# Experts by triples of feature blocks, converted weights kept in DRAM, pairs begun with four single blocks

## The chip, the cores and the metric

The kernel runs on one core of one Trainium2 chip. The metric is the device time of one execution in microseconds (us). Three executions of the kernel before took 2083.7 (median), 2082.83 and 2087.57 us.

## The reference

Three stages, of which the last is the one that changes:

```python
x = attention(r, k, v, w, u)          # 4 x 8 heads, 768 steps, 48 wide -> 3072 tokens x 384
x = (h * tanh(softplus(h))) @ w_out   # h = x @ w_in, 384 -> 2048 -> 384
logits = x @ w_gate                   # 8 experts
P = exp(logits - logits.max())
for _ in range(8):                    # rows, then columns, made to sum up evenly
    P /= P.sum(1, keepdims=True) + 1e-09
    P /= P.sum(0, keepdims=True) + 1e-09
    P *= N / E
for e in range(8):
    out += P[:, e:e + 1] * (relu(x @ w1[e]) @ w2[e])   # 384 -> 1024 -> 384
```

Everything is float32, and the output is 3072 x 384.

## The kernel before

Tokens lie in six tiles of 512, features on partitions: `xT[n]` holds a tile as three blocks (`KI`) of 128 features. The expert stage takes two tiles at a time, a pair q = 0, 1, 2. A float32 product of a 128 x 128 weight block and a 128 x 512 token block is made of three matmuls on parts of the operands (`PASSES`: high x high, high x low, low x high), so each operand is split first: ACT copies the rounded high part, POOL or DVE subtracts it from the source for the low part. In the middle of the program, therefore, every block of x and every weight exists as a high and a low tile.

Per pair, the hidden features of the eight experts (8 blocks of 128 each, 64 in all) are done in groups of two blocks (`groups`, 96 of them). The products of a group are 2 token tiles x 2 feature blocks x 3 input blocks, 12 by themselves; with sums of weights (`w_sums`, L797 to L800) and sums of x (`x_sum`) the group needs 11, in 8 steps, on two banks of PSUM, `U_` and `Bk` (`p1`, `prod`, L846). After each step the bank is read out: by ACT (`c_out`, L868) or by DVE with a sum (L871), with one sum on POOL (L873). Four finished hidden tiles per group are rectified and split, high by ACT (`c_hi`, L879), low by DVE (`c_lo`, L885).

The second layer's matmuls of the group before (`y_part`, L893) are issued between those steps: six after an even step, three after an odd one, into six more banks `Y`. At the end of an expert, DVE weights each of the six banks with that expert's P (L909; `pb` is P laid out over partitions) and POOL adds it to the output tile, which takes the place of x in `xT` (`y_out`, L910). Expert 0 of pair 0 is copied out unweighted (L903) since P is not ready, and weighted later (L1122).

Each group loads four raw weight tiles of 192 KB (`load_w`, L775, on SP's queue), in each pair anew. ACT and POOL split them (`w_hi` L784, `w2_hi` L804, `w_lo` L790). Between pairs, the nine blocks and sums of x are split anew (`x_split`, L840 on ACT and L841 on DVE), at steps of a table at the end of the builder. The order on every engine is the order of the calls in `step`: `step_pe` (products, the entries of `slot`, the second layer's matmuls) and then `step_rest` (weights of the next groups, read-outs, splits, outputs, the entries of `aux`).

The first group's steps are put between the last iterations of the mish layer (`lead`, `ready`), whose result is evacuated at L340. The logits of the last tile are made after that: three differences on DVE (L1088) give the low parts for its matmuls. After the last group come `tail_out` and `tail_turn`, which weight and turn the last two tiles.

## Time and profile before

| | |
|---|---|
| median of three executions | 2083.7 us |
| the profiled execution | 2087.63 us |
| its span | 2085.8 us |
| granted clock of TensorE, mean | 0.993 |
| busy: TensorE, DVE, ACT, POOL | 98%, 62%, 56%, 54% |
| mean rate of the DMA queues | 70 GB/s |

The profile is of one execution by itself, 3.9 us above the median; its own time stands beside its span, and the runs are compared with each other. In it PE is TensorE, DVE is VectorE, ACT is ScalarE, POOL is GpSimd, and SP issues the DMAs. A line such as L871 is a line of the kernel. The granted clock is the share of full speed that the chip allows TensorE in a stretch (1.00 is 2.4 GHz). The expert stage runs from about 549 us to the end.

### The profile page before, as it was taken

The numbers are of one execution on the slowest core, as the hardware profiler recorded it, in microseconds if no ns is written. First come the engines' busy times: TensorE is split into PE (matmuls) and PEld (weight loads), VectorE is DVE, ScalarE is ACT, GpSimd is POOL, SyncE is SP. The second block draws the span as 40 slices with busy tenths as digits, with TensorE's granted clock in tenths as the row PEclk, the third lists the DMA queues.
The fourth block names the chain that finished last, engine by engine and source line by source line (L and its number), as shares of the span: only waits on it lengthen the run. The fifth ranks groups of instructions, "written<-read, shape, count | busy, mean of one in ns | idle before, by whom it ended". The sixth has DMA issues, their size and how long they took to land.

```text
span 2085.8 us, 27895 instructions
## 1 busy us (share of the span) xinstructions
PE 2052.8 (98%) x9586; PEld 1695.8 (81%) x9586; DVE 1286.1 (62%) x2219; ACT 1167.5 (56%) x2486; POOL 1128.6 (54%) x979
## 2 busy tenths in 40 slices
PE   8899999999999999999999999999999999999998
PEld 7888888888788888888878888888878888888887
DVE  8988789778766555445574445555466454455554
ACT  7888888878644444444444555555544444444442
POOL 5546566446534665555564456555566455555651
PEclk8999999999999999999999999999999999999999
...
GB/s 255 211 141 29 33 23 46 16 1 16 25 51 63 67 60 48 62 64 64 56 68 97 96 94 90 101 76 87 93 56 90 64 50 56 65 62 60 60 50 47
DMA packets 127689, 145.56 MB, mean 70 GB/s; under 512 B 35056, under 2 KB 113584, under 8 KB 127536
## 3 DMA queue, kind: packets, MB, share of 16 engines
...
q14 instruction: 76, 0.62, 0.1%
HBM read 138.82 MB, written 4.82 MB: 69 GB/s over the span
## 4 chain that ended last, share of the span: by engine, by line
PE 92%; DVE 3%; ACT 2%; issue 1%; POOL 1%; DMA 0%; POOLq 0%; DVEq 0%; ACTq 0%
PE y L893 37%; PE Bk L846 21%; PE U L846 12%; PE ph L239 9%; PE x L324 9%; PE ya L643 1%; PE un L614 1%; PE sc L602 1%; ACT A L594 1%; PE ya L641 1%; DVE A L607 0%; DVE tc L871 0%; ACT xT L654 0%; POOL wc L790 0%; POOL g L313 0%
## 5 line engine op out<-in xcount | busy, mean ns | idle before, releaser
L893 PE MATMUL y<-g,w 128*128 128x512 f32 x3456 | 911.3, 390 | 0.0
L893 PEld LDWEIGHTS y<-g,w 128*128 128x128 f32 x3456 | 646.2, 188 | 140.7 <-DVE tc L909 7.3
L879 ACT ACTIVATE g<-tc 128x512 fp32r<-128x512 f32 x384 | 242.7, 632 | 651.3 <-DVE tc L871 651.3
L871 DVE TENSOR_TENSOR tc<-Bk,tc 128x512 f32<-128x512 f32 x288 | 199.0, 691 | 571.7 <-PE Bk L846 566.6
L790 POOL TENSOR_TENSOR wc<-er,wc 128x384 fp32r<-128x384 f32 x192 | 212.6, 1107 | 418.8 <-ACT wc L784 418.8
L885 DVE SCALAR_TENSOR_TENSOR g<-tc,g 128x512 fp32r<-128x512 f32 x384 | 309.3, 805 | 60.4 <-ACT g L879 59.8
L846 PE MATMUL Bk<-xc_X,wc 128*128 128x512 f32 x864 | 244.0, 390 | 0.6 <-POOL xc_X L841 0.6
L790 POOL TENSOR_TENSOR w<-er,w 128x384 fp32r<-128x384 f32 x192 | 210.4, 1112 | 56.5 <-ACT w L804 51.8
L324 PE MATMUL x<-g,wm 128*128 128x512 f32 x864 | 212.4, 390 | 0.4 <-POOL g L313 0.2
L239 PE MATMUL ph<-xs,wm 128*128 128x512 f32 x864 | 212.0, 390 | 0.3 <-POOL xs L209 0.3
L910 POOL TENSOR_TENSOR xT<-xT,tc 128x512 f32<-128x512 f32 x120 | 164.2, 1392 | 86.8 <-DVE tc L909 75.1
L873 POOL TENSOR_TENSOR tc<-tc 128x512 f32<-128x512 f32 x96 | 133.2, 1387 | 120.9 <-ACT tc L868 116.8
L239 PEld LDWEIGHTS ph<-xs,wm 128*128 128x128 f32 x864 | 161.8, 188 | 36.6 <-POOL xs L209 0.7
L846 PEld LDWEIGHTS Bk<-xc_X,wc 128*128 128x128 f32 x864 | 162.4, 188 | 35.5 <-POOL xc_X L841 1.0
L324 PEld LDWEIGHTS x<-g,wm 128*128 128x128 f32 x864 | 161.6, 188 | 35.8 <-POOL g L313 1.1
L313 POOL TENSOR_TENSOR g<-y,g 128x512 fp32r<-128x512 f32 x96 | 125.0, 1302 | 113.3 <-ACT g L308 106.6
L868 ACT ACTIVATE tc<-U 128x512 f32<-128x512 f32 x288 | 169.8, 590 | 26.7 <-PE U L846 21.5
L846 PE MATMUL U<-xh,wc 128*128 128x512 f32 x576 | 162.4, 390 | 0.6 <-DVE tc L871 0.6
L846 PE MATMUL Bk<-xc_B,wc 128*128 128x512 f32 x576 | 161.7, 389 | 0.0
L846 PEld LDWEIGHTS U<-xh,wc 128*128 128x128 f32 x576 | 108.1, 188 | 24.7 <-DVE tc L871 1.5
L846 PEld LDWEIGHTS Bk<-xc_B,wc 128*128 128x128 f32 x576 | 108.1, 188 | 22.5
L784 ACT ACTIVATE wc<-er 128x384 fp32r<-128x384 f32 x192 | 99.3, 517 | 45.0 <-DVE er L800 45.0
...
## 6 DMA issues: line engine op xcount, KB each, us to landing
er<-in_w_dram SPq DMA_DIRECT2D x384, 192.0 KB, 2.4
...
lt<-in_kr_dram SPq DMA_DIRECT2D x24, 384.0 KB, 5.7
raw<-in_w_in_dram SPq DMA_DIRECT2D x16, 384.0 KB, 3.3
raw<-in_w_out_dram SPq DMA_DIRECT2D x16, 384.0 KB, 3.1
seen<-in_w_in_dram SPq DMA_DIRECT2D x16, 384.0 KB, 3.5
seen<-in_w_out_dram SPq DMA_DIRECT2D x16, 384.0 KB, 3.2
```

Of the source, the lines that this page charges most:

```text
L239: pe.matmul(ph, w[:, pw, k, :], xs[:, px, :], start=(m == 0), stop=(m == 3 * KI - 1))
L313: pool.tensor_tensor(gs[i][:, 1], y, gs[i][:, 0].bitcast(F32), op=ALU.subtract)
L324: pe.matmul(sums[n][k], wo[f][:, pw, k, :], g[:, px, :], start=(f == f0 and m == 0), stop=(f == f1 and m == 1), skip_group_check=True)
L790: eng.tensor_tensor(flat(t[:, 1]), src, flat(t[:, 0]).bitcast(F32), op=ALU.subtract)
L846: pe.matmul(out_, w[:, pw, :], x[px], start=(start and m == 0), stop=(stop and m == 2), skip_group_check=True)
L868: act.activation(tt[("t0", "t5", "t2", 0, "t3")[s]], Bk if s == 1 else U_, AF.Copy)
L871: dve.tensor_tensor(t, U_ if s == 6 else Bk, t, op=ALU.add)
L873: pool.tensor_tensor(tt["t2"], tt["t2"], tt["t5"], op=ALU.add)
L879: act.activation(g[:, 0], tt[nm], AF.Relu)
L885: dve.scalar_tensor_tensor(g[:, 1], tt[nm], 0.0, g[:, 0].bitcast(F32), op0=ALU.max, op1=ALU.subtract)
L893: pe.matmul(Y[t][k], w2[G, f][:, pw, k, :], x[:, px, :], start=(g == 0 and f == 0 and m == 0), stop=(g == NGR - 1 and f == 1 and m == 2), ...
L910: pool.tensor_tensor(o, o, t_, op=ALU.add)
```

## The change

The 64 feature blocks of a pair are taken as four single blocks and twenty triples, without regard to where an expert ends (`groups`). A single block has 3 steps: 6 products without any weight sums (`T1`). A triple is 2 token tiles x 3 feature blocks x 3 input blocks in 15 products and 15 steps (`T3`): every product is one step, the two banks take turns, and each bank keeps adding up over its products, so that what is read out after a step is a partial sum. A row of `T3` names the product, whether its bank starts anew, how it is read out (c copied, n copied with its sign turned, both by ACT at L925; + and - added to or taken from a hidden tile by DVE at L927; L929 is that of the single blocks), and to which of the tiles. Six of the fifteen read-outs finish a hidden tile. Its low half (L1019) is not issued in its own step but in the next one, behind that step's read-out (`pend`). Five places are kept for hidden tiles.

The second layer's matmuls are given out as jobs of three (`job`, L1027) by a plan made when the kernel is built (`plan_jobs`): a smooth curve of jobs per step between what is finished two steps before and what must be done for a place to come free.

Weights are converted in pair 0 only. Every converted tile (high and low, 384 KB) is written to DRAM (`w_keep`, L855: eight for a triple, two for a single block, 168 in all) and read back for pairs 1 and 2 (`w_back`, L859, 336 loads). Sums of weights (`w_sums`, L820) are 10 DVE operations a triple.

The fifteen x operands need more room: two tiles of x are saved to DRAM and read back later, pair 2 is worked on in the first two tiles. The first three experts of pair 0 are written to DRAM without weights (L1047), read back in pair 1 and weighted and added on POOL. At a pair change the operands are made anew in an order of their own (`refill`, with `x_split` at L881 and L882 and `x_neg` at L889).

```diff
-NGR = NF2 // 2
+NB = E * NF2
+NSG = 4
+NTR = (NB - NSG) // 3
+GQ = NSG + NTR
+NPK = 3
+NGB = 5
...
-    XN = ("B11", "T1", "T2", "B21", "X31", "T3", "B22", "X32", "T4")
-    WN = ("A11", "A12", "A13", "S4", "A22", "A23", "S1", "S2", "S3")
-    groups = [(q, e, g) for q in range(NQ) for e in range(E) for g in range(NGR)]
...
+    T3 = ((14, 1, "c", "00"), (2, 1, "c", "21"), (12, 0, "c", "10"), (4, 1, "c", "11"), (13, 1, "+", "10"),
+          (7, 1, "-", "21"), (6, 0, "-", "11"), (1, 0, "-", "11"), (5, 0, "-", "21"), (0, 0, "+", "10"),
+          (11, 0, "n", "01"), (8, 0, "+", "00"), (9, 0, "+", "00"), (3, 0, "-", "01"), (10, 0, "c", "20"))
+    DONE = {7: "11", 8: "21", 9: "10", 12: "00", 13: "01", 14: "20"}
+    T1 = (((("a0", 5), ("a2", 1)), 1, "c", 1), ((("a0", 9), ("a1", 12), ("a2", 14)), 1, "-", 0), ((("a1", 4),), 0, "c", 1))
+    ROW = {"1": 0, "2": 1, "0": 2}
+    TI = {"00": 0, "21": 1, "10": 2, "11": 3, "01": 3, "20": 2}
+    groups = [
+        (q, fs) for q in range(NQ) for fs in [(f,) for f in range(NSG)] + [(f, f + 1, f + 2) for f in range(NSG, NB, 3)]]
...
+    def w_keep(G, i, second, t, z):
+        fs = groups[G][1]
+        d = kept[fs, i, second] = dr.tile([128, 2, KI, 128], F32, name=f"keep{fs[0]}_{i}_{int(second)}")
+        at_z(z, lambda: nc.sync.dma_start(d, t.bitcast(F32)))
+    def w_back(G, i, second):
+        if G < NGT:
+            nc.sync.dma_start(w_new(G, i, second).bitcast(F32), kept[groups[G][1], i, second])
...
+    def x_neg(o, x, y):
+        dve.scalar_tensor_tensor(o, x, -1.0, y, op0=ALU.mult, op1=ALU.subtract)
...
-    STEPS = ((("S1", "T1"),), (("A12", "B21"), ("A13", "X31")), (("S4", "B22"), ("A13", "X32")),
-             (("A22", "T4"), ("A23", "X31")))
-    STEPU = (("A11", "B11"), ("S2", "T2"), ("S3", "T3"), ("A23", "X32"))
...
+    banks, cnt, used = [None, None], [0], {}
+    def steps(G):
+        return T3 if full(G) else T1
     def p1(G, s):
+        b = banks[cnt[0] & 1]
+        sb[0] = banks[1 - (cnt[0] & 1)]
+        cnt[0] += 1
+        used[G, s] = b
+        if full(G):
+            p, start, _, _ = T3[s]
+            prod(b, G, p, p, start, True)
         else:
+            ps_, start, _, _ = T1[s]
+            for j, (wn, xn) in enumerate(ps_):
+                prod(b, G, wn, xn, start and j == 0, j == len(ps_) - 1)
+    def evac(G, s):
+        b = used.pop((G, s))
+        if full(G):
+            _, _, kind, o = T3[s]
+            t = tmp["c", TI[o]]
         else:
+            _, _, kind, o = T1[s]
+            t = tmp["c", 2 * (G % 2) + o]
+        if kind in "cn":
+            act.activation(t, b, AF.Copy, scale=1.0 if kind == "c" else -1.0)
+        elif full(G):
+            dve.tensor_tensor(t, t, b, op=ALU.add if kind == "+" else ALU.subtract)
+        else:
+            dve.tensor_tensor(t, b, tmp["c", 2 * (G % 2) + 1], op=ALU.subtract)
+        f = done_(G, s)
+        return (t,) + f if f else None
...
+    def c_hi(G, t, f, tok):
+        q = groups[G][0]
+        g = gfix[gslot[q, f, tok]]
+        act.activation(g[:, 0], t, AF.Relu)
+        gg[q, f, tok] = g
+        return lambda: dve.scalar_tensor_tensor(g[:, 1], t, 0.0, g[:, 0].bitcast(F32), op0=ALU.max, op1=ALU.subtract)
...
+        if q == 0 and e < NPK:
+            d = raws[e, t, k] = dr.tile([128, TT], F32, name=f"yraw{e}_{t}_{k}")
+            act.activation(t_, yo, AF.Copy)
+            nc.sync.dma_start(d, t_)
...
+        p1(G, s)
+        for fn in slot.pop((G, s), ()):
+            fn()
+        while jp[0] < jq[zi[G, s]]:
+            job(*jobs[jp[0]])
+            jp[0] += 1
...
+        done = evac(G, s)
+        for fn in pend:
+            fn()
+        pend.clear()
+        if done:
+            if gfix:
+                pend.append(c_hi(G, *done))
+            else:
+                early.append((G, *done))
...
+        on(0, 7, sp(13, "C", dve))
+        on(0, 8, sp(1, b[2][1], pool))
+        on(0, 9, sp(5, b[0][1], pool))
+        on(0, 10, lambda: x_neg(x_tmp("D"), tmp["C"], b[2][1]))
+        on(0, 10, sp(7, "D", dve))
+        on(0, 11, tt("A", b[1][0], "A", ALU.subtract))
+        on(0, 11, neg("D", "C", b[0][1]))
+        on(0, 12, sp(6, "D", dve))
+        on(0, 13, sp(9, "B", pool))
```

Three places in the order of instructions. First, TensorE in the steady part of a pair. Before, L846 is the first layer (U and Bk are its banks, `wc` weights, the others x) and L893 the second (y):

```order
L893 MATMUL y_5781<-g_5_7739,w_15_0_7599 128x512 x3
L846 MATMUL Bk<-xc_B_5395,wc_0_7675 128x512 x3
L846 MATMUL Bk<-xc_X_5435,wc_0_7675 128x512 x3
L893 MATMUL y_5782<-g_5_7739,w_15_0_7599 128x512 x3
L846 MATMUL U<-xc_T_5528,wc_2_7702 128x512 x3
L893 MATMUL y_5777<-g_7_7769,w_15_1_7617 128x512 x3
L893 MATMUL y_5778<-g_7_7769,w_15_1_7617 128x512 x3
L846 MATMUL Bk<-xc_B_5651,wc_1_7688 128x512 x3
L846 MATMUL Bk<-xc_X_5689,wc_0_7675 128x512 x3
```

After it, L895 is the first layer and L1027 a job of the second:

```order
L895 MATMUL U<-hB,wc_4_10144 128x512 x3
L1027 MATMUL y_5816<-gf_5820,w_0_10019 128x512 x3
L895 MATMUL Bk<-hC,wc_4_10144 128x512 x3
L1027 MATMUL y_5817<-gf_5820,w_0_10019 128x512 x3
L895 MATMUL U<-xc_5715,wc_3_10129 128x512 x3
L1027 MATMUL y_5812<-gf_5818,w_0_10019 128x512 x3
L895 MATMUL Bk<-xc_5759,wc_0_10105 128x512 x3
L1027 MATMUL y_5813<-gf_5818,w_0_10019 128x512 x3
L895 MATMUL U<-xc_5790,wc_4_10144 128x512 x3
L1027 MATMUL y_5814<-gf_5818,w_0_10019 128x512 x3
```

Between two uses of the same bank by different steps there were 12 or 15 matmuls of other work and there are now 9 or 12, and a bank is read out after three matmuls each time, where `Bk` mostly was after six.

Second, DVE at the hand-over from the mish layer (L340 and L347 read out its last result; L389, L392, L396 and L399 are the logits; L885 and L1019 low halves; L871 read-outs). Before:

```order
L340 TENSOR_TENSOR xT_78<-half_3501,x_4_8_0_5452 128x512
L340 TENSOR_TENSOR xT_78<-half_3501,x_4_8_1_5453 128x512
L340 TENSOR_TENSOR xT_78<-half_3501,x_4_8_2_5454 128x512
L389 STREAM_TRANSPOSE gt_5741<-g_4378 32x512
L392 TENSOR_TENSOR lg<-gt_5741 32x32 x4
L871 TENSOR_TENSOR tc_5576<-Bk,tc_5576 128x512
L871 TENSOR_TENSOR tc_5576<-U,tc_5576 128x512
L885 SCALAR_TENSOR_TENSOR g_5_5749<-tc_5576,g_5_5749 128x512
L871 TENSOR_TENSOR tc_5577<-Bk,tc_5577 128x512
L885 SCALAR_TENSOR_TENSOR g_6_5785<-tc_5576,g_6_5785 128x512
```

After it, L882 is a split of x and L1360 the gate differences:

```order
L347 TENSOR_TENSOR xT_92<-half_3505,x_4_8_0_5463 128x512
L347 TENSOR_TENSOR xT_92<-half_3505,x_4_8_1_5464 128x512
L347 TENSOR_TENSOR xT_92<-half_3505,x_4_8_2_5465 128x512
L396 STREAM_TRANSPOSE gt_5783<-g_4382 32x512
L399 TENSOR_TENSOR lg<-gt_5783 32x32 x4
L882 TENSOR_TENSOR xc_5790<-xt_D,xc_5790 128x512
L1019 SCALAR_TENSOR_TENSOR gf_5818<-tc_5629,gf_5818 128x512
L1019 SCALAR_TENSOR_TENSOR gf_5819<-tc_5630,gf_5819 128x512
L1019 SCALAR_TENSOR_TENSOR gf_5820<-tc_5631,gf_5820 128x512
L1019 SCALAR_TENSOR_TENSOR ge_5821<-tc_5632,ge_5821 128x512
L1360 TENSOR_TENSOR xg_1_5835<-xT_92,xg_0_5834 128x512
L1360 TENSOR_TENSOR xg_1_5839<-xT_92,xg_0_5838 128x512
```

A split, four low halves (`gf` and `ge` are the places of hidden tiles) and the gate differences now stand there in a row.

Third, DVE at the change from pair 0 to pair 1. Before (L841 splits of x, L871 read-outs, L885 low halves):

```order
L885 SCALAR_TENSOR_TENSOR g_3_13778<-tc_5576,g_3_13778 128x512
L841 TENSOR_TENSOR xc_B_5395<-xT_78,xc_B_5395 128x512
L871 TENSOR_TENSOR tc_5576<-Bk,tc_5576 128x512
L841 TENSOR_TENSOR xc_T_5528<-xt_T_13745,xc_T_5528 128x512
L871 TENSOR_TENSOR tc_5576<-U,tc_5576 128x512
L885 SCALAR_TENSOR_TENSOR g_5_13816<-tc_5576,g_5_13816 128x512
L841 TENSOR_TENSOR xc_B_5651<-xT_79,xc_B_5651 128x512
L871 TENSOR_TENSOR tc_5577<-Bk,tc_5577 128x512
```

After it (L882 splits of x, L889 its sums, L927 read-outs, L1019 low halves):

```order
L927 TENSOR_TENSOR tc_5632<-tc_5632,Bk 128x512
L927 TENSOR_TENSOR tc_5632<-tc_5632,U 128x512
L882 TENSOR_TENSOR xc_5715<-xt_C,xc_5715 128x512
L927 TENSOR_TENSOR tc_5630<-tc_5630,Bk 128x512
L1019 SCALAR_TENSOR_TENSOR ge_5822<-tc_5632,ge_5822 128x512
L927 TENSOR_TENSOR tc_5631<-tc_5631,U 128x512
L1019 SCALAR_TENSOR_TENSOR ge_5821<-tc_5630,ge_5821 128x512
L1019 SCALAR_TENSOR_TENSOR gf_5820<-tc_5631,gf_5820 128x512
L889 SCALAR_TENSOR_TENSOR xt_D<-xt_C,xT_91 128x512
L882 TENSOR_TENSOR xc_5759<-xt_D,xc_5759 128x512
```

A split stood ahead of nearly every read-out there. Now splits and sums stand in a few places of the last triple, ahead of read-outs and of low halves.

## Rows read from the trace of the kernel before

**Rows 1.** Page: busy time by engine; chain that ended last, by engine and line.

```profile
PE 2052.8 (98%) x9586; PEld 1695.8 (81%) x9586; DVE 1286.1 (62%) x2219; ACT 1167.5 (56%) x2486; POOL 1128.6 (54%) x979
...
PE 92%; DVE 3%; ACT 2%; issue 1%; POOL 1%; DMA 0%; POOLq 0%; DVEq 0%; ACTq 0%
PE y L893 37%; PE Bk L846 21%; PE U L846 12%; PE ph L239 9%; PE x L324 9%; PE ya L643 1%; PE un L614 1%; PE sc L602 1%; ACT A L594 1%; PE ya L641 1%; DVE A L607 0%; DVE tc L871 0%; ACT xT L654 0%; POOL wc L790 0%; POOL g L313 0%
```

**Rows 2.** Table of stretches: length, busy us (count) by engine, clock, DMA share, GB/s.

```profile
0.00:52.00 52.00, 42.91 (x338) 38.99 (x338) 45.90 (x84) 37.66 (x120) 30.12 (x43) 0.87 0.90 255
541.15:556.15 15.00, 14.28 (x62) 11.05 (x61) 7.96 (x13) 10.13 (x21) 12.01 (x11) 1.00 0.12 32
556.15:564.00 7.85, 4.82 (x15) 3.59 (x14) 5.95 (x13) 1.55 (x3) 0.95 (x3) 0.78 0.00 1
1055.00:1085.00 30.00, 29.51 (x126) 22.85 (x125) 25.79 (x38) 14.85 (x29) 19.38 (x16) 1.00 0.21 47
1085.00:1555.00 470.00, 470.00 (x2068) 387.38 (x2067) 236.16 (x407) 246.18 (x522) 253.40 (x220) 1.00 0.32 90
1555.00:1590.00 35.00, 33.99 (x144) 26.22 (x143) 29.43 (x41) 16.57 (x34) 24.20 (x20) 1.00 0.21 48
```

**Rows 3.** TensorE's waits from 580 to 2064 us: total us, times, longest us.

```profile
PE Bk L846 <- DVE tc L871: 1.4, 4, 0.5
PE U L846 <- DVE tc L871: 0.6, 2, 0.3
```

**Rows 4.** Page, groups of instructions: busy us, mean ns of one, idle before.

```profile
L871 DVE TENSOR_TENSOR tc<-Bk,tc 128x512 f32<-128x512 f32 x288 | 199.0, 691 | 571.7 <-PE Bk L846 566.6
L790 POOL TENSOR_TENSOR wc<-er,wc 128x384 fp32r<-128x384 f32 x192 | 212.6, 1107 | 418.8 <-ACT wc L784 418.8
L885 DVE SCALAR_TENSOR_TENSOR g<-tc,g 128x512 fp32r<-128x512 f32 x384 | 309.3, 805 | 60.4 <-ACT g L879 59.8
...
L910 POOL TENSOR_TENSOR xT<-xT,tc 128x512 f32<-128x512 f32 x120 | 164.2, 1392 | 86.8 <-DVE tc L909 75.1
...
L868 ACT ACTIVATE tc<-U 128x512 f32<-128x512 f32 x288 | 169.8, 590 | 26.7 <-PE U L846 21.5
```

**Rows 5.** Timeline of TensorE at the hand-over: start us, us, instruction, idle before.

```profile
560.02 1.62 PE L846 MATMUL Bk<-xc_T,wc 128*128 128x512 f32 x3 [3.03 <-DVE tc L871]
```

**Rows 6.** Timeline of DVE at the hand-over.

```profile
555.85 1.88 DVE L340 TENSOR_TENSOR xT<-half,x 128x512 f32<-128x512 f32 x3 [3.96 <-PE x L324]
557.65 0.69 DVE L389 STREAM_TRANSPOSE gt<-g 32x512 f32<-32x512 f32 x1
558.38 0.77 DVE L392 TENSOR_TENSOR lg<-gt 32x32 f32<-32x32 f32 x4
...
565.70 2.72 DVE L1088 TENSOR_TENSOR xg<-xT,xg 128x512 fp32r<-128x512 f32 x3
```

**Rows 7.** Timeline of DVE at the first pair change, a split of x.

```profile
1057.20 0.69 DVE L841 TENSOR_TENSOR xc_B<-xT,xc_B 128x512 fp32r<-128x512 f32 x1 [0.62 <-ACT xc_B L840]
```

**Rows 8.** Instructions of line L841: min/median/max ns, first and last start us.

```profile
L841 DVE TENSOR_TENSOR xc_B<-xT,xc_B x4: 693/1236/1780, 1050.9 to 1562.1; 128x512 fp32r<-128x512 f32 x4
L841 DVE TENSOR_TENSOR xc_T<-xt_T,xc_T x4: 837/1308/1778, 1054.5 to 1568.2; 128x512 fp32r<-128x512 f32 x4
```

**Rows 9.** Timeline of TensorE in a steady group, from 703 us.

```profile
703.18 0.84 PE L846 MATMUL Bk<-xc_B,wc 128*128 128x512 f32 x3
703.86 0.84 PE L846 MATMUL Bk<-xc_X,wc 128*128 128x512 f32 x3
704.54 0.84 PE L893 MATMUL y<-g,w 128*128 128x512 f32 x3
```

**Rows 10.** Timeline of DVE in the same group.

```profile
704.81 0.69 DVE L871 TENSOR_TENSOR tc<-Bk,tc 128x512 f32<-128x512 f32 x1 [1.67 <-PE Bk L846]
706.10 0.69 DVE L871 TENSOR_TENSOR tc<-U,tc 128x512 f32<-128x512 f32 x1 [0.60 <-PE U L846]
706.71 1.05 DVE L885 SCALAR_TENSOR_TENSOR g<-tc,g 128x512 fp32r<-128x512 f32 x1
```

**Rows 11.** Chain that ended last, its piece at 2064 us: start us, us.

```profile
2064.29 6.12 PE y L893 x27
```

**Rows 12.** Page, DMA issues: count, KB each, median us to landing.

```profile
raw<-in_w_in_dram SPq DMA_DIRECT2D x16, 384.0 KB, 3.3
```

More of the change, by code (lines that the diff above doesn't have):

```diff
@@ L913, in layers, with at_z @@
     slot, aux = {}, {}
+    pend, late, wq = [], {}, []
+    def at_z(z, fn):
+        late.setdefault(z, []).append(fn)
     def step(G, s):
@@ L1000, in layers @@
     hf = ctx.enter_context(tc.tile_pool(name="hf", bufs=NT - 1, side="right"))
+    dr = ctx.enter_context(tc.tile_pool(name="dr", bufs=1, space=bass.MemoryType.DRAM))
+    xsave = [dr.tile([128, KI, TT], F32, name=f"xsave{i}") for i in range(2)]
     with mst:
@@ L1081, in at_ @@
         d.setdefault((G, s), []).append(fn)
+    gfix.extend(gpl.tile([128, 2, TT], F32R, name=f"gf{i}", tag="g") for i in range(NG))
+    gfix.extend(ge.tile([128, 2, TT], F32R, name=f"ge{i}", tag="g") for i in range(NGB - NG))
+    for x in early:
+        c_hi(*x)()
+    hx["E"] = hf_tile("hE")
+    home[3] = hx["E"][:, 0, :], hx["E"][:, 1, :]
+    home[10] = hx["D"][:, 2, :], hx["E"][:, 2, :]
+    xs_home(8)
+    xs_home(11)
     def gate_last(k):
@@ L1222, in tail_dma @@
         nc.sync.dma_start(out[r0:r0 + 128, :], ot[2 * t + i // 2][:, i % 2, :])
-    y_part(G, 1, range(KI))
-    for k in range(KI):
-        y_part(G, 3, (k,))
-        tail_out(1, k)
-    for k in range(KI):
-        y_part(G, 0, (k,))
-        y_part(G, 2, (k,))
-        tail_out(0, k)
-        tail_turn(1, k)
+    rest = jobs[jp[0]:]
+    for x in rest:
+        job(*x)
+        _, f, t, k = x
+        if f == NB - 1 and t == 1:
+            tail_out(1, k)
+        elif f == NB - 2 and t == 0:
+            tail_out(0, k)
+            tail_turn(1, k)
     for i in range(NSUB):
```

687 lines of the change are left out of this document (456 added, 231 removed).

## The prediction

> **What bounds the kernel now.** I read the busy shares and the chain of waits first. TensorE is busy 98% of the span and holds 92% of the chain, with the expert stage's second layer (L893), then its first layer's products (L846), as the largest lines [rows 1]. So time goes as the matmuls do, unless a change opens waits between them. The table of stretches then gives a price: in the middle of the expert stage TensorE is busy for all of 470.00 us at granted clock 1.00, with 2068 matmuls, so 470.00 / 2068 = 0.2273 us each; the same table shows where it is not so, at the hand-over from the mish layer (541 to 564 us) and at the two pair changes (around 1060 and 1570 us) [rows 2]. The table of waits says the rest: from 580 to 2064 us TensorE waits 2.0 us in all for evacuations of its two banks [rows 3]. There is nothing else to win in that stage than matmuls, and all that the change adds to waits is loss.
>
> **What is removed.** The first layer of an expert goes from 33 matmuls for two blocks (96 groups, 3168) to 45 for three (60 triples) and 18 for a single block (12 singles): 60 x 45 + 12 x 18 = 2916. The second layer stays at 3456. That is 252 matmuls fewer, all on the chain: 252 x 0.2273 = 57.3 us. The conversions of weights of pairs 1 and 2 go too: on POOL 1.1 us each (L790) [rows 4], and their halves on ACT and the sums on DVE. I cost that at nothing: TensorE waits on none of them in steady state [rows 3], so what hides them is TensorE's own 98%.
>
> **What is added, on the path.** Five terms.
>
> (1) *Hand-over.* Before, 62 + 15 matmuls take 15.00 + 7.85 us [rows 2]; at 0.2273 they would take 17.5, so 5.3 us are lost there, 3.03 of it in one wait for L871 [rows 5]. After the change the first job of the second layer needs the second of four early low halves (L1019), and DVE comes to it through three x evacuations (1.88 us for the three), a transpose and four additions to the logits (0.7 + 0.77), a split of x, and that low half behind another; after the two further low halves the three gate differences (2.72 us) stand ahead of the next evacuation [rows 6]. Taken from the last mish matmul: 1.9 + 1.5 + 1.1 + 1.4 = 5.9 us, less the 1.4 us of the six matmuls that TensorE still has, is 4.5 us of waiting; the gate differences add some 1 us, and the low clock of that place (0.78 [rows 2]) 2 to 3. Some 8 us instead of 5.3 is 2.7 more by a count that leaves out two evacuations of 0.69 us between these: I take +4, with bounds 0 (the old loss again) and 8 (all of it new).
>
> (2) *Pair changes.* Before, 126 and 144 matmuls fill 30.00 and 35.00 us [rows 2], that is 1.4 and 2.3 us lost. After it DVE has a split of x in its queue ahead of an evacuation and of the low half that the next job needs. A split waits for ACT (0.62 us in the trace) and takes 0.69 us at its best and up to 1.78, with medians of 1.24 and 1.31 [rows 7, 8]: about 1.9 us. A job that needs a low half behind such a split has no slack (term 3 makes it 0.2 us late without one) and waits 2.1 us; a bank hides 1.1 of the 1.9 (term 4) and waits 0.8. One place of each kind per change gives 2.9, two changes 5.8, against 3.7 before: 2.1 more. I take +4, since what is late on DVE there also pushes the low halves behind it; bounds 0 and 10 (every split at 1.78 us, nothing hidden).
>
> (3) *Jobs two steps behind.* In the last triples of pairs 0 and 1 the plan gives out jobs two steps behind their product. The products on Bk of one step end at 704.54 us, where the second layer's matmuls begin; their evacuation ends at 705.50 and the low half at 707.76, behind another evacuation. That is 3.2 us with a low half of 1.05 us, 2.9 with one of 0.69 [rows 9, 10]; two steps give about 3.0. So it is up to 0.2 us late in some ten triples: +2, bounds 0 and 4.
>
> (4) *Two banks, one product at a time.* Now each product is evacuated by itself and the two banks alternate. A step is three matmuls of a product and one or two jobs: 45 + 54 = 99 matmuls for 15 steps, 6.6 or 1.50 us on average and 1.36 us at least, where before 69 matmuls for 8 steps gave 1.96 us. The evacuation must fit into what lies between two uses of a bank: the jobs behind the product, the other bank's product and its jobs. That is 2.05 us at the least (3 + 3 + 3 matmuls), and 0.96 is used: 0.27 us after the product's end at 704.54 L871 begins, and it takes 0.69 us [rows 9, 10]; ACT's takes 0.59 (L868) [rows 4]. So 1.1 us are left, and a low half of 0.69 us ahead of it on DVE fits. Low halves take 0.81 us on average (L885) [rows 4] and 1.05 at 706.71 us [rows 10]: with one such the 1.1 are gone. Per triple DVE has 9 evacuations and 6 low halves, 9 x 0.69 + 6 x 0.81 = 11.1 us of 22.5, so queues are short. I take 0.05 us per triple, +3; bounds 0 and 8.
>
> (5) *Pair 1's extra work*: y of three experts comes back from DRAM and is weighted on POOL (1.39 us for a 128x512, as L910 takes now [rows 4], in no wait of TensorE [rows 3]), and shares three buffers with the evacuations of y. +2, bounds 0 and 5.
>
> The tail keeps its order: 27 matmuls in 6.12 us, then the turns [rows 11]. 0.
>
> **What I cost at nothing.** The transfers. In pair 0 a triple writes eight tiles of 0.393 MB and reads six of 0.197: 4.3 MB, with the y tiles up to 4.9, in 22.5 us, or 190 to 218 GB/s. The start of the kernel moved 255 GB/s with the DMA engines 90% busy, in steady state it is 90 [rows 2]. In pairs 1 and 2 a triple reads 3.1 MB, 140 GB/s. A tile read back is asked for at least 75 matmuls (17 us) before its first use, and a 384 KB load lands in 3.3 us [rows 12]. What hides them is that lead; were it gone, each of 336 loads could cost up to its 3.3 us.
>
> **The sum.** -57.3 + 4 + 4 + 2 + 3 + 2 = -42.3 us. The profiled execution took 2087.6 us, 3.9 above the median of the three runs (2083.7). Against the profile the sum gives 2045.3; against the median **2041.4 us**. With all bounds at the good end it is 2026.4, at the bad end (35 us) 2061.
>
> **A rule that speaks against it.** In this trace TensorE cycles through banks already, two of them for the first layer and six for the second, at granted clock 1.00 over 470 us; the clock is lower (0.78) only around a wait of 3.03 us [rows 2, 5]. The Trainium skill, "TensorE: Matmul & The Clock Gate", section "A second HAM failure mode: psum-queue depth-cycling", says that a kernel which cycles through banks of PSUM and leaves TensorE briefly idle between groups of matmuls can see its clock swing between the two levels, so that throughput falls though a single matmul does not. By that rule more and shorter turns of two banks are a risk; by the rows they are none as long as the waits stay a fraction of a microsecond. By the rule the sum would take on the 380 us of rival D at worst; it goes by the rows.
>
> **Rivals.**
> - *Only the count* (A): evacuations and splits fit everywhere. 2083.7 - 57.3 = 2026.4 us. For it: 2.0 us of waits in 1484 us [rows 3]. Against it: the DVE queue at the hand-over and at pair changes. 0.10.
> - *Two banks bind in steady state* (B): a low half stretched to 1.05 us and an evacuation behind it use up the 1.1 us some three times a triple, with 0.17 us each: 60 x 0.5 = 30 us in place of term 4's 3, 2041.4 + 27 = 2068, or 2058 to 2075. For it: the six short waits on L871 that exist already, with nearly a third more time per step (1.96 us) [rows 3]. 0.15.
> - *Pair 0's transfers* (C), the one that ends slower: SP issues stores and raw loads in one queue, stores wait for POOL's low halves, loads stand behind them. Pair 0 moves 168 x 0.393 + 128 x 0.197 + 18 x 0.262 = 96 MB in 2124 matmuls' 483 us, 199 GB/s. Where DMA gives less than 96 MB / (483 + 46) us = 181 GB/s for this mix, the gain is gone: at 175 GB/s pair 0 takes 549 us, 66 more, and the time is 2107 us. Against it: 255 GB/s at the start, though those were mostly loads [rows 2]. 0.05.
> - *The clock swings* (D): many short waits of TensorE bring the granted clock down again and again, to the 0.78 of the stretch around the 3.03-us wait. At 0.78 for whole triples 22.5 us would be 28.8, and 60 x 6.3 = 380 us more, some 2420 us. Only that one stretch speaks for it [rows 2]. 0.02. (It is what the Trainium skill's section above would lead to.)
> - That the matmuls do not go away is excluded: the order of instructions has 252 fewer.
>
> **How the numbers follow.** The forecast, 2030 to 2058 us, has the remaining 0.68. About 0.2% (4 us) is what a measurement of this kernel can tell from no change. Forecast, A and B end faster, all but a sliver: faster 0.92, same 0.02, slower 0.06. The range runs from A's 2026 to 2065, past the sum of the bad ends and half of B; C, D and the rest of B, some 0.15, lie outside.
>
> **What would show it.** Step 1: some 6372 expert matmuls, at 0.227 us in a stretch of 470 us. Terms 1 and 2: waits of TensorE for DVE in the windows of the hand-over and the pair changes, at 8 and 3.4 us each. Term 4 against B: waits of products on U and Bk for the new evacuations summed over the triples, 3 us or 30. C: waits of TensorE or ACT on DMA in pair 0, with a DMA share near 0.9. D: granted clock below 1.00 in stretches without a long wait. The prediction is wrong if triples take more than 22.5 us by over 0.4, or if pair 0 is longer than pair 2 by more than 10 us.

## The result and the profile after

The changed kernel takes 2049.5 us (median of four runs, 2047.08 to 2052.63), the kernel before, run beside it, 2085.6 (2082.83 to 2087.65). The ratio of the two is 0.9829, interval 0.9808 to 0.9849. It is 36.1 us faster; 42.3 were forecast, and 2041.4 us, with a range that holds the result.

The page of the changed kernel, busy time by engine, against [rows 1]:

```profile
PE 1997.0 (98%) x9334; PEld 1648.0 (81%) x9334; DVE 1376.0 (67%) x2185; ACT 1062.4 (52%) x2204; POOL 745.3 (36%) x631
```

9586 - 9334 = 252 matmuls are gone, as counted. DVE has become busier, though two pairs' weight sums left it: it now reads out nine of fifteen steps of a triple.

The table of stretches of the changed kernel (length, busy us of TensorE and its matmuls, granted clock, DMA share, GB/s), against [rows 2]:

```profile
541.11:554.87 13.76, 13.20 (x58) 1.00 0.08 24
554.87:562.55 7.68, 2.61 (x9) 0.73 0.42 121
562.55:568.68 6.13, 6.13 (x14) 0.50 1.02 404
568.68:580.00 11.32, 11.32 (x51) 1.00 0.48 181
580.00:1000.00 420.00, 412.55 (x1813) 1.00 0.58 201
1000.00:1060.00 60.00, 56.07 (x236) 0.97 0.58 198
1060.00:1500.00 440.00, 436.67 (x1922) 1.00 0.59 190
1500.00:1550.00 50.00, 48.33 (x209) 1.00 0.38 122
1550.00:2020.00 470.00, 469.09 (x2068) 1.00 0.48 148
```

The last row holds as many matmuls in 470 us as the kernel before had between its pair changes [rows 2]: triples with two alternating banks run at the full price of 0.2273 us a matmul. What a stretch takes beyond its matmuls at that price is lost time (a row is good to some 2 us: the 1855 matmuls that the kernel before has from 580 to 1000 us come out at 421.6 us, which is entered as 0):

| place | before | after | more | forecast |
|---|---|---|---|---|
| hand-over, to 580 us | 5.0 | 8.9 | +3.9 | +4 (term 1) |
| pair 0, to 1000 us | 0 | 7.9 | +7.9 | +3 for all pairs (term 4), +2 (term 3) |
| first pair change, to 1060 | 1.4 | 6.4 | +5.0 | +4 for both (term 2) |
| pair 1, to 1500 | 0 | 3.1 | +3.1 | +2 (term 5) |
| second pair change, to 1550 | 2.3 | 2.5 | +0.2 | |
| pair 2, to 2020 | 0 | 0 | 0 | |

That is 20 us more than before instead of 15, and -57.3 + 20.1 = -37.2 against the measured -36.1.

Four kinds of waits make it up. First, pair 0: the timeline of DVE in a triple with a Sinkhorn iteration (one of the eight rounds that make the rows and columns of P sum up evenly), then of TensorE (start us, us, operation; in brackets the idle time before it and what ended it):

```profile
598.53 0.34 DVE L423 TENSOR_REDUCE rs<-Pm 128x24 f32<-128x192 f32 x1
598.90 0.61 DVE L424 TENSOR_SCALAR rs<-rs 128x24 f32<-128x24 f32 x1
599.55 0.30 DVE L425 RECIPROCAL rs<-rs 128x24 f32<-128x24 f32 x1
599.88 0.78 DVE L426 TENSOR_TENSOR Pm<-Pm,rs 128x192 f32<-128x192 f32 x1
600.70 0.52 DVE L428 TENSOR_REDUCE cs<-Pm 128x8 f32<-128x192 f32 x1
601.13 0.69 DVE L927 TENSOR_TENSOR tc<-tc,Bk 128x512 f32<-128x512 f32 x1
...
601.88 0.96 PE L895 MATMUL Bk<-hE,wc 128*128 128x512 f32 x3 [0.59 <-DVE tc L927]
```

From 598.53 to 601.13 a read-out stands behind 2.6 us of other work, and the product that needs its bank waits 0.59 us. It is so in seven of the eight triples, and twice a read-out stands behind weight sums (L820) and a weighted output (L1049), with waits of 0.81 and 1.82 us. The longer of the two, on DVE and on TensorE:

```profile
938.04 1.62 DVE L820 TENSOR_TENSOR r<-r,sw 128x128 f32<-128x128 f32 x2
...
940.55 0.68 DVE L1049 TENSOR_TENSOR xT<-y,pb 128x512 f32<-128x512 f32 x1
941.15 0.68 DVE L927 TENSOR_TENSOR tc<-tc,Bk 128x512 f32<-128x512 f32 x1
```

```profile
941.88 0.96 PE L895 MATMUL Bk<-xc,wc 128*128 128x512 f32 x3 [1.82 <-DVE tc L927]
```

TensorE's waits from 580 to 990 us (total us, times, longest) are these and nothing else, but for 0.4 us for the transpose of P:

```profile
PE Bk L895 <- DVE tc L927: 3.6, 4, 1.8
PE U L895 <- DVE tc L927: 3.5, 5, 0.9
```

Second, POOL at the end of pair 0 (timeline of POOL):

```profile
995.03 8.82 POOL L1050 TENSOR_TENSOR xT<-xT,xT 128x512 f32<-128x512 f32 x6 [1.23 <-DVE xT L1049]
1003.82 2.58 POOL L841 TENSOR_TENSOR wc<-r,wc 128x384 fp32r<-128x384 f32 x2
```

Six additions of outputs stand ahead of two low halves of weights, and TensorE waits 2.27 us for one of them at 1005.31; after it the clock falls to half for a few matmuls. Third, pair 1 (timeline of DVE, then of TensorE):

```profile
1376.46 0.69 DVE L1049 TENSOR_TENSOR xT<-y,pb 128x512 f32<-128x512 f32 x1 [3.57 <-DMA out_dram<-xT]
```

```profile
1378.41 0.96 PE L895 MATMUL Bk<-hE,wc 128*128 128x512 f32 x3 [2.48 <-DVE tc L927]
```

DVE wants to write one of the three buffers of outputs while the transfers of a turned output still read it. Fourth, the hand-over (timeline of TensorE), against [rows 5]:

```profile
556.72 0.50 PE L895 MATMUL U<-x5r,wc 128*128 128x512 f32 x1 [1.23 <-POOL wc L841]
...
558.98 0.80 PE L1027 MATMUL y<-gf,w 128*128 128x512 f32 x1 [1.06 <-ACT gf L1017]
562.55 0.80 PE L1027 MATMUL y<-gf,w 128*128 128x512 f32 x1 [2.78 <-DVE gf L1019]
```

and 6.13 us at clock 0.50 behind them. (This execution had a low clock there: from 541 to 580 us the mean granted clock is 0.87, and 0.91 in sums_pool and pool_order, whose code at this place is the same.) The pair changes add the jobs' waits for low halves, 0.95 us each.

### The profile page after: what moved, and what is told of

The parts are those of the page before. It is cut to its first block, busy times and chain, and to the rows that moved or that the text cites. A ratio compares the mean times of both kernels' runs of the same rounds, so it can differ in the third digit from the quotient of the medians.

```text
span 2046.2 us, 27338 instructions
## 1 busy us (share of the span) xinstructions
PE 1997.0 (98%) x9334; PEld 1648.0 (81%) x9334; DVE 1376.0 (67%) x2185; ACT 1062.4 (52%) x2204; POOL 745.3 (36%) x631
## 4 chain that ended last, share of the span: by engine, by line
PE 87%; DVE 7%; ACT 2%; issue 2%; POOL 1%; DMA 0%; SPq 0%; DVEq 0%; POOLq 0%; ACTq 0%
PE y L1027 35%; PE Bk L895 15%; PE U L895 15%; PE ph L246 9%; PE x L331 9%; DVE tc L927 1%; DVE gf L1019 1%; PE ya L649 1%; PE un L620 1%; PE sc L608 1%; ACT A L600 1%; DVE ge L1019 1%; PE ya L647 0%; DVE A L613 0%; DVE xc L882 0%
## 5 line engine op out<-in xcount | busy, mean ns | idle before, releaser
L1027 PE MATMUL y<-gf,w 128*128 128x512 f32 x2088 | 572.6, 391 | 4.8 <-DVE gf L1019 3.7
L1027 PEld LDWEIGHTS y<-gf,w 128*128 128x128 f32 x2088 | 391.6, 188 | 88.4 <-DVE gf L1019 5.5
L1027 PE MATMUL y<-ge,w 128*128 128x512 f32 x1368 | 375.0, 391 | 0.9 <-DVE ge L1019 0.9
L1017 ACT ACTIVATE gf<-tc 128x512 fp32r<-128x512 f32 x232 | 146.4, 632 | 403.7 <-DVE tc L927 391.6
L927 DVE TENSOR_TENSOR tc<-tc,Bk 128x512 f32<-128x512 f32 x270 | 185.1, 686 | 236.5 <-PE Bk L895 222.8
L927 DVE TENSOR_TENSOR tc<-tc,U 128x512 f32<-128x512 f32 x270 | 185.4, 687 | 222.8 <-PE U L895 208.5
L1027 PEld LDWEIGHTS y<-ge,w 128*128 128x128 f32 x1368 | 256.9, 188 | 55.1 <-DVE ge L1019 1.9
L1019 DVE SCALAR_TENSOR_TENSOR gf<-tc,gf 128x512 fp32r<-128x512 f32 x232 | 193.3, 837 | 20.7 <-ACT gf L1017 15.8
L331 PEld LDWEIGHTS x<-g,wm 128*128 128x128 f32 x864 | 161.6, 188 | 36.1 <-POOL g L320 1.6
L925 ACT ACTIVATE tc<-U 128x512 f32<-128x512 f32 x192 | 114.3, 595 | 85.9 <-PE U L895 80.2
L925 ACT ACTIVATE tc<-Bk 128x512 f32<-128x512 f32 x192 | 114.2, 595 | 85.2 <-PE Bk L895 79.1
L895 PE MATMUL Bk<-xc,wc 128*128 128x512 f32 x540 | 152.5, 390 | 4.6 <-DVE tc L927 2.3
L895 PE MATMUL U<-xc,wc 128*128 128x512 f32 x540 | 151.9, 389 | 0.8 <-DVE tc L927 0.8
L1019 DVE SCALAR_TENSOR_TENSOR ge<-tc,ge 128x512 fp32r<-128x512 f32 x152 | 126.2, 832 | 21.0 <-ACT ge L1017 15.4
L841 POOL TENSOR_TENSOR w<-r,w 128x384 fp32r<-128x384 f32 x64 | 68.6, 1076 | 156.3 <-ACT w L840 146.6
L895 PEld LDWEIGHTS Bk<-xc,wc 128*128 128x128 f32 x540 | 101.0, 188 | 27.3 <-DVE tc L927 3.4
```

What stands on the lines that cost most here:

```text
L331: pe.matmul(sums[n][k], wo[f][:, pw, k, :], g[:, px, :], start=(f == f0 and m == 0), stop=(f == f1 and m == 1), skip_group_check=True)
L841: eng.tensor_tensor(flat(t[:, 1]), src, flat(t[:, 0]).bitcast(F32), op=ALU.subtract)
L895: pe.matmul(out_, w[:, pw, :], x[px], start=bool(start and m == 0), stop=bool(stop and m == 2), skip_group_check=True)
L925: act.activation(t, b, AF.Copy, scale=1.0 if kind == "c" else -1.0)
L927: dve.tensor_tensor(t, t, b, op=ALU.add if kind == "+" else ALU.subtract)
L1017: act.activation(g[:, 0], t, AF.Relu)
```

## The experiments

All are made from the changed kernel; their times stand beside its 2049.5 us. They were run in several sets, and the kernel before, run beside each, had medians from 2083.5 to 2086.4 us. In the profiles the fourth-last group of mish matmuls, ahead of nearly all that the edits touch, starts anywhere from 537.6 us (pair_turn) to 545.0 (sink_early). So a difference of some 3 us from 2049.5 is no evidence by itself. Of the edits made alone only the sums on POOL, with or without the Sinkhorn halves, have an interval of the ratio clear of the changed kernel's; for the others the waits and the stretches of their own place decide.

**Weight sums on POOL**

```diff
-                w_sums(H, s)
+                w_sums(H, s, pool)
                 if s == 2:
-                    w_sums(H, 3)
+                    w_sums(H, 3, pool)
```

> The ten weight sums of a triple (L820) move from DVE to POOL in pair 0; nothing else changes. Theory: two waits of the changed kernel in pair 0 (0.81 us at 871.61, 1.82 us at 941.88) come from an evacuation that stands on DVE behind sums and weighted outputs, and go, 2.6 us; the 0.6-us waits once a triple from 601 to 767 us come from the first half of a Sinkhorn iteration and stay: about 2047 us where the changed kernel has 2049.5. Rival, POOL is then late with the halves of the weights (8 splits of 1.06 us and some 4 us of sums in a triple of 22.5 us): new waits of products for L841 after outputs, and 2050 us or more.

Measured: 2042.2 us (2041.33 to 2043.51). The two waits behind sums and outputs are gone; the seven Sinkhorn waits are there, at 0.58 to 1.03 us. The gain of 7 us is more than the 2.6 us of those waits. In the profiles another part, 1.7 us, is the clock, and it is luck: the wait for the late weight is 2.27 us in both kernels, yet here the clock stays at 1.00 behind it, and in the changed kernel it does not. Where the rest comes from is not shown. Table of stretches, the changed kernel's row first:

```profile
1005.30:1012.00 6.70, 6.69 (x22) 0.75 0.81 280
```

```profile
1003.00:1010.00 7.00, 7.00 (x33) 1.00 0.67 226
```

**Sinkhorn's halves at other steps**

```diff
-    at_(slot, NSG, 3, lambda: smax_c(stage["m"]))
+    at_(slot, NSG, 0, lambda: smax_c(stage["m"]))
...
-        at_(aux, NSG + i, 10, lambda i=i: stage.update(c=sink_a(i)))
-        at_(slot, NSG + i, 14, lambda i=i: sink_b(i, stage["c"]))
+        at_(aux, NSG + i, 1, lambda i=i: stage.update(c=sink_a(i)))
+        at_(slot, NSG + i, 10, lambda i=i: sink_b(i, stage["c"]))
```

> As sums_pool, and the first half of each Sinkhorn iteration moves from step 10 to step 1 of its triple, the second from 14 to 10, where the read-outs are ACT's. Theory: in the changed kernel that half takes 2.6 us on DVE ahead of an evacuation, more than the 1.1 us of slack plus a step without a DVE read-out, which costs 0.58 to 0.89 us in seven of eight triples, 4.5 us; all of them go, so about 4.5 us less than sums_pool, 2042.5. Rival, it is the low halves of hidden tiles stretched by POOL (up to 1.4 us) that make DVE late: then waits of about 0.6 us a triple stay, also behind triples without an iteration, and the time is that of sums_pool.

Measured: 2042.9 us, with six waits of 0.47 to 0.89 us at the same place. That fits the rival's number, but not its reason: on DVE the second half now stood there, 2.5 us from 597.26 to 599.80, with a low half of 1.22 us behind it. In this kernel the matmul of the second half also writes into a bank that still holds partial sums, so it computes other values of P; it tells only where DVE is late. So the second half went back.

```diff
-        at_(slot, NSG + i, 10, lambda i=i: sink_b(i, stage["c"]))
+        at_(slot, NSG + i, 14, lambda i=i: sink_b(i, stage["c"]))
```

> As sums_pool, with the first half of each Sinkhorn iteration in step 1 of its triple, and the second left in step 14 (in sums_pool_sink it stood in step 10, where its matmul used a bank in which partial sums still stood, so that run's Sinkhorn values and outputs are not the reference's). Theory: both halves then stand where the read-outs are ACT's, DVE takes neither of them ahead of an evacuation, and the seven waits of 0.58 to 1.03 us from 601 to 767 us go: 4.6 us less than sums_pool's 2042.2, some 2038. Rival, low halves stretched by POOL are what makes DVE late at that step: waits of 0.5 us and more stay.

Measured: 2037.9 us (2033.03 to 2039.34), the forecast of the theory. From 600 to 1000 us two waits are left, the late weight among them:

```profile
PE Bk L895 <- POOL wc L841: 2.3, 1, 2.3
PE U L366 <- ACT pt L367: 0.4, 1, 0.4
```

Low halves still take up to 1.45 us there (at 600.07), so their length alone makes no read-out late.

**Splits of weights between outputs on POOL**

```diff
-            k = len(wq) if s in (2, 14) else (0 if busy or (3 <= s < 5) else 1)
+            k = len(wq) if s in (2, 14) else (0 if 3 <= s < 5 else 1)
```

> One split of a weight per step goes on in steps that also give out weighted outputs, where the changed kernel holds splits back. Theory: the wait of 2.27 us at 1005.31 is for a weight half (L841) that stands on POOL behind six additions of outputs (8.82 us from 995.03); with the splits between them it goes, and with it the stretch of lower clock after it (0.97 from 1000 to 1050 us, worth some 2.2 us): about 4 us less than the changed kernel, 2045.5. Rival, the additions are late instead and with them the three buffers of outputs, so that evacuations of y wait on DVE: waits of 1 to 2 us at the same place, and no gain.

Measured: 2046.9 us, 2.6 less, where some 4 were forecast. From 1000 to 1080 us there are 332 matmuls at clock 1.00 instead of 321 at 0.98, which is 2.5 us. The wait for the late weight is gone; a wait of 1.4 us for DVE is there in its place, so theory and rival each had half:

```profile
PE U L895 <- DVE tc L927: 2.0, 2, 1.4
```

**Pair 2 converts its weights**

```diff
+        j = G - 2 * GQ - NSG
+        if j >= 0 and G < NGT - 1 or j == NTR - 1:
+            c0, c1, c2 = j >= 2, j >= 1 and H < NGT, j >= 0 and G + 2 < NGT
+            conv(G, s, busy, c0, c1, c2)
...
+            if G >= 2 * GQ + NSG + 1:
+                continue
```

`conv` is pair 0's schedule of loads, sums and splits without the stores; the second piece leaves out the reads.

> In pair 2, 18 of the 20 triples convert their weights anew (raw loads, sums on DVE, halves on ACT and POOL) as pair 0 does; the cached tiles are read back for the four single blocks and two triples alone. It measures what the cached weights of one pair are worth. Theory of the prediction: nothing, since TensorE's time covers the conversions: the stretch from 1550 to 2020 us stays at 470 us with under 2 us of waits, and the time is within 2 us of the changed kernel's 2049.5. Rival: what pair 0 shows besides its Sinkhorn waits (two evacuations late behind sums and outputs, 2.6 us, and one late weight, 2.3 us with a clock dip behind it) comes back in pair 2, at 2 to 7 us: 2052 to 2057, so that the cached weights are worth that much per pair.

Measured: 2059.1 us (2052.46 to 2059.68), 9.6 more for one pair and more than the rival's 2 to 7; by the two ratios (0.9861 and 0.9829) it is 6.7. The table of stretches says that the loss lies in pair 2, the changed kernel's row first:

```profile
1560.00:2020.00 460.00, 459.09 (x2025) 1.00 0.48 147
```

```profile
1560.00:2020.00 460.00, 452.14 (x1975) 1.00 0.27 71
```

50 matmuls fewer are 11.4 us in this execution, the slowest of the four. TensorE's waits from 1640 to 2030 us:

```profile
PE U L897 <- POOL wc L841: 2.9, 2, 2.7
PE Bk L897 <- DVE tc L929: 2.4, 3, 1.3
PE U L897 <- DVE tc L929: 1.7, 1, 1.7
```

They are pair 0's waits again, 7.0 us, and the clock is 0.98 behind the longest (1960 to 2035 us). In this order the cached weights are worth some 7 to 10 us a pair, where the prediction had nothing.

**Every tile stored twice**

```diff
-        at_z(z, lambda: nc.sync.dma_start(d, t.bitcast(F32)))
+        d2 = dr.tile([128, 2, KI, 128], F32, name=f"keeq{fs[0]}_{i}_{int(second)}")
+        at_z(z, lambda: (nc.sync.dma_start(d, t.bitcast(F32)), nc.sync.dma_start(d2, t.bitcast(F32))))
```

> Every converted tile is stored to DRAM twice in pair 0 (168 more stores of 0.393 MB, 66 MB), the second copy unused. It tests the transfers of pair 0. The prediction's view: stores are hidden behind TensorE as long as the rate stays under what the DMA engines can give, which the start of the kernel puts at 255 GB/s or more; pair 0 would want some 162 MB in 485 us, 334 GB/s, so either the engines give that (a slice of the output writes reached 403) and the time stays within 3 us of 2049.5, or pair 0 grows to 162 MB / 255 GB/s = 635 us, 150 us more. Rival, SP's queue is the limit and not the bytes: loads behind the doubled stores are late in single steps, with waits on DMA summing to 5 to 40 us.

Measured: 2052.5 us, 3.0 more. The table of stretches for pair 0, the run's row and the changed kernel's above:

```profile
580.00:1000.00 420.00, 411.28 (x1805) 1.00 0.91 336
```

336 GB/s with the engines 91% busy, and 8 matmuls (1.8 us) fewer in 420 us than with 201 GB/s. So the transfers of pair 0 were far from their limit, and the condition of the prediction's rival C, less than 181 GB/s for this mix, is not met. The rival named for this run had its late loads: from 580 to 1000 us ACT waits 56.6 us in all for raw weights, 17.2 in the changed kernel. But TensorE waits for no transfer there in either.

**The hand-over**

```diff
-            x_split(6, tmp["D"], dve)
...
-        if z in (13, 14, 15):
+        if z in (13, 14):
             w_split(NSG, z - 13, pool, zi[2, 0])
+        elif z == 15:
+            w_split(2, 0, pool, zi[2, 0])
+            w2_split(2, 0, pool, zi[2, 0])
...
+    at_(aux, 2, 1, lambda: x_split(6, tmp["D"], dve))
```

> At the hand-over alone: the third split of x on DVE moves behind the four early low halves and the gate differences, and the weights of single block 2 are split on POOL before those of the first triple. Theory: the wait of 1.23 us for that weight goes, and 0.69 us of the 2.78 us wait for the second low half; with less than 5.6 us of waits the stretch at granted clock 0.50 (6.1 us, about 3 us lost) may shrink or stay: 2 to 5 us less than the changed kernel's 2049.5. Rival, what is taken from the front of DVE's queue comes back behind it: the splits of x for the singles and the first triple are late then, with waits of 1 us or more from 570 to 590 us, and no gain.

Measured: 2052.6 us, 3.0 more. The waits for the weight and for ACT are gone, but two others took their place (timeline of TensorE):

```profile
561.86 0.47 PE L1027 MATMUL y<-gf,w 128*128 128x512 f32 x1 [2.25 <-DVE xT L347]
565.82 2.50 PE L1027 MATMUL y<-gf,w 128*128 128x512 f32 x5 [3.49 <-DVE gf L1019]
```

They come to 5.7 us, as much as the waits from 554 to 563 us in the changed kernel did (5.6 with one of 0.56 us for POOL): the read-out of the mish result and the low half came no sooner behind the last mish matmul, and TensorE only stopped at other places. The mish layer was not held back by this edit, though the next expectation says so: its last matmuls end at 558 us where they ended at 555, but the whole execution ran 4 us late by then, and from the fourth-last group of mish matmuls (543.13 us here, 539.07 in the changed kernel) to the end of the last it took 15.1 us, not 16.0. A second edit left the weights alone, took DVE's x work out of the last mish iterations, and with it POOL's split of product 0:

```diff
-            x_split(13, tmp["C"], dve)
-            x_neg(tmp["D"], tmp["C"], b[2][1])
...
-            x_split(0, tmp["A"], pool)
...
-            x_split(7, tmp["D"], dve)
-            x_neg(tmp["D"], tmp["C"], b[0][1])
...
-            x_split(6, tmp["D"], dve)
...
-    at_(aux, 2, 0, lambda: pool.tensor_tensor(tmp["C"], b_[2][0], tmp["C"], op=ALU.subtract))
...
+    at_(aux, 2, 0, lambda: x_split(13, tmp["C"], pool))
+    at_(aux, 2, 0, lambda: x_neg(x_tmp("D"), tmp["C"], b_[2][1]))
+    at_(aux, 2, 0, lambda: x_split(7, tmp["D"], pool))
...
+    at_(aux, 2, 1, lambda: x_neg(x_tmp("E"), tmp["C"], b_[0][1]))
+    at_(aux, 2, 1, lambda: x_split(6, tmp["E"], pool))
+    at_(aux, 2, 2, lambda: x_split(0, tmp["A"], pool))
+    at_(aux, 2, 2, lambda: pool.tensor_tensor(tmp["C"], b_[2][0], tmp["C"], op=ALU.subtract))
```

> At the hand-over alone, in place of hand_over (which held back the mish layer: weights split on POOL ahead of its products made its last matmuls 3.9 us later): the three x splits and two sums that DVE does among the last mish iterations (7.1 us of DVE time from 549.10 to 557.14 and 560.60) go behind the low halves and gate differences, the splits to POOL. Theory: DVE reaches the evacuations of the mish result as soon as they are there, 1.4 us earlier, and the low half 0.7 us earlier still, so the wait of 2.78 us shrinks by 2 us: 2 to 4 us less than the changed kernel's 2049.5 (the more if the stretch at clock 0.50 shrinks). Rival, what sets the place is ACT and POOL with the last mish tile and the weights of single block 2 (waits of 1.23 and 1.06 us): these stay, the low half is no earlier, and the time is 2049.5.

Measured: 2044.9 us (2042.34 to 2050.65), 4.7 less, with a wide spread. The waits of 1.23 and 1.06 us are gone with it, which neither side had expected: in the changed kernel a high half of x (L881) stood on ACT at 557.25, ahead of those of the hidden tiles, and waited 1.71 us for DVE's sum; and POOL had a split of 1.30 us (L882 at 553.97) ahead of the weight. The wait for the low half is still 2.6 us, but it ends 4.3 us behind the last mish matmul instead of 7.5, and a new one of 2.3 us stands at the maximum of the logits (L405):

```profile
PE y L1027 <- DVE gf L1019: 2.6, 1, 2.6
PE U L410 <- DVE m L405: 2.3, 1, 2.3
```

**Turned outputs and the pair changes**

```diff
-        o = ytmp[k]
+        o = mr.tile([128, TT], F32, name=f"tn{n}_{k}", tag="raw")
...
-        on(0, 7, sp(13, "C", dve))
+        on(0, 7, sp(13, "C", pool))
...
```

and the same for products 7 and 6.

> Two edits at different places. (a) Turned outputs of a pair get buffers of their own instead of the three that the weighted outputs of an expert use. Theory: the 2.48-us wait at 1378.41 (DVE held 3.57 us at 1376.46 for a transfer out of such a buffer) and the 0.49 us before it go. (b) The three x splits on DVE at a pair change go to POOL. Theory: the waits at 1043.49 and 1050.39 (0.95 and 0.71) and at 1532.27 and 1539.17 (the same) go, 3.3 us. Together 6 us less than the changed kernel's 2049.5: 2043.5. Rival to (b): POOL, at 1.3 us for a split and with outputs' additions before it, is later than DVE, and first-layer products wait for POOL at the pair changes, 2 us or more each.

Measured: 2045.9 us, 3.6 less, where 6 were forecast; by the ratios (0.9823 and 0.9829) it is 1.3. (a) held: from 1080 to 1500 us 0.5 us of waits are left. (b) held by half: the four waits are gone, and one of 1.3 us stands in each pair change. The timeline of DVE shows why:

```profile
1048.09 1.76 DVE L889 SCALAR_TENSOR_TENSOR xt_D<-xt_C,xT 128x512 f32<-128x512 f32 x1 [1.47 <-POOL xc L882]
1049.77 0.67 DVE L927 TENSOR_TENSOR tc<-tc,Bk 128x512 f32<-128x512 f32 x1
```

The second sum of x is written over the first, which POOL has to split before; the read-out stands behind it. The next kernel gives it a buffer of its own.

**All of them**

`four_edits` has the sums on POOL, the early Sinkhorn half, the splits between outputs, the turned outputs' buffers, and the pair changes on POOL with the second sum in `x_tmp("E")`; `five_edits` adds the second edit of the hand-over.

> Together: weight sums on POOL, first half of a Sinkhorn iteration in step 1, splits between outputs on POOL, turned outputs in buffers of their own, x splits of a pair change on POOL with a buffer of its own for the second sum (in pair_turn it waited 1.47 us for POOL to have read the first, and an evacuation behind it 1.32 us). Theory: the waits are separate, so the gains add: sink_early's 2037.9, less 2.3 us and a clock dip of some 2 us of the late weight at 1000 us, less 1.9 us of the turned outputs, less 3.3 us of the two pair changes: 2028 to 2031 us. Rival, POOL is the next bound, with splits, sums, x splits and outputs in pair 0's last triples: waits for L841 or L882 of 2 us and more there, and 2034 us or more.

> four_edits and the edit of hand_over2. Theory: another 2 to 4 us less than four_edits, 2025 to 2028 us, close to what the count of matmuls alone gives (2026.4 on the scale of a median of 2083.7). Rival: as of hand_over2, no gain over four_edits.

Measured: 2028.1 us (2025.73 to 2029.16; ratio 0.9723, interval 0.971 to 0.9736) and 2025.2 us (2023.47 to 2026.87; ratio 0.9709, interval 0.9695 to 0.9722). The gains of `four_edits`, 21.4 us, are about the sum of what its parts gave alone (11.6, 2.6 and 3.6) and of the two waits of 1.3 us that pair_turn had left. What the fifth edit adds, 2.9 us by the medians, is not settled: the intervals overlap, and in the two profiles the stretch from the fourth-last group of mish matmuls to the end takes 1485.6 us in both. The table of stretches of `four_edits`:

```profile
580.00:1000.00 420.00, 419.57 (x1857) 1.00 0.59 203
1000.00:1080.00 80.00, 78.50 (x343) 1.00 0.64 203
1080.00:1500.00 420.00, 419.52 (x1848) 1.00 0.60 189
```

Pair 0 and pair 1 now hold 1857 and 1848 matmuls in 420 us, what pair 2 always had (420 / 0.2273 = 1848).

**Is the cache still worth anything?** `five_edits` with pair 2 converting as above, sums on POOL and splits between outputs.

> five_edits, and in pair 2 the conversions of 18 triples again (as convert_pair2, but with the sums on POOL, splits between outputs, and the turned outputs of pair 1 in the three shared buffers, since the others hold raw weights). It tells what of the 9.6 us that convert_pair2 cost were the sums on DVE. Theory: convert_pair2 lost it to evacuations behind sums and outputs on DVE (4.1 us of waits), to a late weight on POOL (2.9 us) and to the clock dip behind that, and POOL and ACT have room for the rest: within 2 us of five_edits' 2025.2, so that with this order cached weights are worth nearly nothing. Rival: the conversions cost by themselves, through operations of POOL that stretch those of DVE and raw loads that come late: 2030 to 2035 us, with waits of 1 us and more for DVE or POOL in pair 2.

Measured: 2029.2 us (2025.57 to 2031.01; ratio 0.9731, interval 0.9716 to 0.9747), 4.1 more, with three waits of 0.35 to 0.93 us for DVE in pair 2 and none for POOL:

```profile
PE Bk L897 <- DVE tc L929: 1.9, 3, 0.9
```

So more than half of what convert_pair2 lost was the order on DVE and POOL; the rest lies between theory and rival. The intervals of the two ratios overlap, so that up to 4 us are left for the cache in one pair is likely, not settled; the waits explain half of them.

## Why the prediction was right, and where it was not

- *What is removed*: right. 252 matmuls fewer, and a stretch of 470 us holds 2068 of them before and after.
- *The conversions taken out of pairs 1 and 2, at nothing*: right for the sum, not for the reason. They cost nothing in the kernel before, whose groups left more time between two uses of a bank; in the new one they cost 7 to 10 us in the pair that has them (convert_pair2). The cover that the prediction named, TensorE's 98%, says nothing of how long a read-out may be late. Without the cache, and with the same order on DVE and POOL, the change would have gained some 17 to 23 us (36.1 less twice 9.6 or 6.7, an estimate from one pair), and pair 0, which has no cache, has waits of the same kind.
- *Term 1, hand-over*: right in size, 3.9 for 4, DVE's queue the longest of the waits. That the size fits is in part luck: the wait for the low half was 2.78 us, not 4.5, and what was not seen are ACT and POOL ahead of it (1.06 and 1.23 us), which went when the x work was moved (hand_over2).
- *Term 2, pair changes*: 5.2 us in the table for 4, but by another cause. That its size fits is luck. The splits on DVE cost 1.7 us of waits a change, about what was lost there before (1.4 and 2.3). 2.27 us and the clock behind it, some 2 us, are the late weight on POOL at the end of pair 0, on which the prediction had no term.
- *Term 3, jobs two steps behind*: nothing. Behind the hand-over the only jobs that wait are those behind the splits at the two pair changes, 0.95 us each, and with the splits they went (pair_turn).
- *Term 4, two banks*: the mechanism was right, its place and size were not. Plain triples wait for nothing, in pair 2 over 470 us. In pair 0 it is 7.1 us, and the step that failed is "9 x 0.69 + 6 x 0.81 = 11.1 us of 22.5, so queues are short": it left out the ten weight sums, the Sinkhorn operations and the weighted outputs, which stand in the same queue in pair 0, and it argued from a sum over a triple where two steps decide. With the weight sums and the first Sinkhorn halves moved, the term is 0 (sink_early). The prediction's own sign of being wrong came here: from the first product of the first triple to the last of the last, the twenty triples take 472.2 us in pair 0 and 450.1 in pair 2, 23.6 and 22.5 us each, and the 29 matmuls that pair 0 has more are at most 6.6 of these 22.1 us. So the forecast of the time held while its picture of pair 0 did not.
- *Term 5, pair 1*: 3.1 for 2, by the three shared buffers as written, but it was the turned outputs' transfers that held them, not the three experts that come back (pair_turn).
- *Rivals.* A, the count alone, is not what the change does, but what it can do: five_edits lies at 2025.2, with before at 2085.9 in the same comparison, 60.7 less. In the two profiles 2.4 us of that lie ahead of the fourth-last group of mish matmuls (541.84 us before, 539.44 here); the 58.3 behind it are about the 57.3 of the count. B did not come: its waits would have stood in every pair. C falls by the 201 GB/s of pair 0 and by keep_twice. D did not come either: over 440 us of pair 1, at two-bank turns of 1.5 us, the granted clock is 1.00. The rule of the Trainium skill, "TensorE: Matmul & The Clock Gate", section "A second HAM failure mode: psum-queue depth-cycling", is not borne out here as far as cycling itself goes; what this trace shows of the expert stage are dips at single waits, those of the hand-over and the 2.27 us at 1005.31, and none behind the 2.48 us at 1378.41 (clock 1.00 from 1378.4 to 1385 us).
